# Masks by TensorE and sums by VectorE for the second batch's local head pairs, with a newly searched order

## The chip, the cores and the metric

The kernel runs on one core of a Trainium2 chip. The metric is the device time in microseconds of one execution of the whole program. A core has five engines with queues of their own: PE (TensorE, matrix products; its weight loads are listed as PEld), DVE (VectorE), ACT (ScalarE), POOL (GpSimd) and SP, which here only issues DMAs. Each engine takes its instructions strictly in the order in which they were emitted.

## What is computed

Eight batches of attention with eight heads each (576 positions, head size 64), and behind it a gated feed-forward block with a spatial product over the positions:

```python
scores = scale * np.matmul(q, k.transpose(0, 1, 3, 2))
mask_local = (rel >= 0) & (rel < stride)                       # stride = 32, heads 0 to 3
mask_strided = (rel >= 0) & (pos[None, :] % stride == pos[:, None] % stride)   # heads 4 to 7
scores = np.where(masks, scores, -1000000000.0)
attn = np.exp(scores - max); attn = attn / (sum(attn) + 1e-09)
x = (attn @ v) with the heads side by side                     # (8, 576, 512)
h = np.maximum(x @ w_in, 0.0); u, v = halves of h
v_n = (v - mean(v)) / np.sqrt(var(v) + 1e-06)
v_s = np.einsum('ts,bsd->btd', w_spatial, v_n) + b_spatial
out = (u * v_s) @ w_out
```

## The kernel before

**Tiles and stages.** Heads are handled in pairs: batch b has four pairs t = 4b to 4b+3, of which the first two are local and the last two strided. `attention(t, due)` (L695) loads q, k and v of a pair and calls `local_attention` (L445) or `strided_attention` (L585). A local pair has 18 blocks of 32 queries by 64 keys, packed into five slots for each of the two heads, so ten slots u of 128x64; the scores (L460) go to two PSUM tiles, one for each head. The result x of a pair (128 x 576, as a rounded and a rest part) feeds `moe_1` (v part: L870, u part: L912), and that feeds `moe_2` (spatial product L993, with the tail rows at L1005 and L1006; projection L1035). Every large product is made of three rounded products, high by high, high by low and low by high, so each weight is split once into a rounded part (`rnd`, L360: L368 on ACT, L370 on DVE or POOL) and a rest (`rest`, L374: L378). w_in and w_out arrive as 64-bit words and are first converted (L746 on ACT, L754 on POOL or L751 on DVE, L762 on DVE).

**Masks and softmax of a local pair.** There are two ways. For pairs in `PE_MASKED`, which are the first batch's four (0 to 3), TensorE adds the masks before the scores (`mask_scores`, L428: minus the unit matrix times the negated masks, L434, from the tile `at_minus`); VectorE takes the maxima of five slots at once (L480), scales them (L488), and ScalarE takes exp straight from PSUM (L517). For the others VectorE adds the mask slot by slot into SBUF, with the maximum as accumulated output (L497, ten instructions, each with a read of the accumulator), and ScalarE takes exp from there. For pairs in `APART` (0 and 1) the sums are a reduction by VectorE (L531); for the others exp writes its sum as well, which adds one accumulator read after each exp. Then come the normalising (L413, L417, L422), a transpose (L541), copies into `ptl` (L368, L370), the product with v (L570) and the split of x (L390 or L392, L378). The strided pairs have their own lines: scores L603, L619 or the mask by TensorE, L628, L634, exp L640, L645, the normalising, L657, copies into `pts`, product L673.

**The order.** Nothing is scheduled by hand. `Program.add` records each operation with a key (a due time in us on a scale of its own; smaller is more urgent), the engines that could do it with a cost in ns, and what it depends on. `Program.order` (L169) plays these through on modelled engines and a modelled DMA (310 bytes per ns, `DMA_RATE`): a free engine takes the ready operation with the smallest key. The engines' instructions are then emitted in the order of the modelled start times, and SP's DMAs too. `KEYS` (L40) holds the keys of the early work: a for the due times of pairs 0 to 7, v and u for the two halves of w_in (four row blocks each), o for w_out, s for the spatial weights, t for their tail, cst for the masks and the unit matrix, fill for the zeroed tiles; lead moves the due times of the pairs from batch 2 on. `fillers` (L280) puts products with zeros (L1168) ahead of PE operations before which the model sees PE idle for over 700 ns.

**Buffers that matter here.** Rings are reused in order, and a user of a slot waits for all earlier users of it: q and k two slots each, v_raw two, the PSUM tiles s two (local pairs from pair 4 on take both), m four, po two, o two. `at_minus`, which holds the negated unit matrix and masks, is the second slot of the ring o, so the second output tile of the first projection waits for the last mask product.

Of the kernel before, what the change touches and what calls it, by code (L numbers as in the profile page):

```python
# [23 lines left out]
STRIDE = 32  # L24
# [13 lines left out]
TAIL = S - 4 * P  # L38
NT = 4
KEYS = {  # L40
    "a": (-1127.3, -1221.6, -672.3, -526.1, 101.7, 33.0, 113.1, 239.5,),
    "v": (-238.9, -1399.6, -76.4, -73.7,),
    "u": (-43.5, -131.3, -12.3, -34.7,),
    "s": (684.8, 251.9, 2902.8, 2024.9,),
    "t": (1654.0,),
    "o": (6.6, -58.9, 103.7, 587.0,),
    "cst": (-1558.0,),
    "lead": (-1.36,),
    "fill": (50.5, 1235.4, -3578.4, 1164.7, -177.7, 809.5,),
    "dp": (849, -9544,),  # L50
    "dpt": (181.75,),
    "near": (198.57,),
}
WARM_END, WARM_GAP, WARM_COST, WARM_COLS, WARM_SHARE = 110000.0, 700.0, 427.0, 256, 0.8
PE_MASKED, APART = (0, 1, 2, 3), (0, 1)
OTHER_BANK = (1, 2, 3)
FETCHED, FETCH_COST = 200.0, 32.0
DMA_RATE = 310.0
# [4 lines left out]
PE, ACT, DVE, POOL, DMA = "tensor", "scalar", "vector", "gpsimd", "sync"  # L63
# [10 lines left out]
def local_blocks(slot):  # L74

    found = {}
    for i, n, first, c0, z in LOCAL_MOVES:  # L80
        if first <= slot < first + n:
            found[z] = 3 * (c0 + slot - first) + i
    return [found[z] for z in range(len(found))]
# [47 lines left out]
class Program:  # L131
# [7 lines left out]
    def add(self, key, choices, fn, reads=(), writes=(), spare=None, tiled=0, port=()):  # L139


        n = len(self.ops)
        if port:
            self.port[n] = port
        if spare is not None:
            self.spare[n] = spare
        if tiled:
            self.tiled[n] = tiled
        deps = set()
        for tok in reads:  # L150
            if tok in self.writer:
                deps.add(self.writer[tok])
            self.readers.setdefault(tok, []).append(n)
        for tok in writes:
            if tok in self.writer:
                deps.add(self.writer[tok])
            deps.update(self.readers.pop(tok, ()))
            self.writer[tok] = n
        for tok in (*reads, *writes):
            buf = tok[0]  # L160
            if isinstance(buf, Buf):
                deps.update(buf.before)
                if buf.n > buf.ring.bufs:
                    deps.update(buf.last.users[:1])
                buf.users.append(n)
        deps.discard(n)
        self.ops.append((key, choices, fn, deps))
# [142 lines left out]
def attention_moe(ctx, tc, qT, kT, vl, vs, cst, eye, w_in, w_out, wsp, wtail, out):  # L310
# [48 lines left out]

    def rnd(key, n, dst, src, reads, writes, engs=(ACT, DVE, POOL), blocks=False):  # L360

        cost = {ACT: 110 + 0.87 * n, DVE: 70 + 0.52 * n, POOL: 110 + 1.75 * n}
        if blocks:
            cost = {ACT: 200 + 0.85 * n, DVE: 175 + 0.5 * n, POOL: 175 + 0.9 * n}

        def fn(eng):
            if hasattr(eng, "activation"):
                eng.copy(dst(), src())  # L368
            else:
                eng.tensor_scalar(dst(), src(), 1.0, 0.0, op0=ALU.mult, op1=ALU.add)  # L370

        add(key, [(e, cost[e]) for e in engs], fn, reads, writes, port=(DVE,))

    def rest(key, n, dst, src, hi, reads, writes, engs=(DVE, POOL), extra=0):  # L374
        cost = {DVE: 70 + 1.04 * n + extra, POOL: 120 + 2.3 * n}

        def fn(eng):
            eng.tensor_tensor(dst(), src(), f32(hi()), op=ALU.subtract)  # L378

        add(  # L380
            key, [(e, cost[e]) for e in engs], fn, reads, writes,
            port=(DVE, POOL) if POOL in engs else (),
        )
# [12 lines left out]
    def load(key, dst, src, writes, nbytes, reads=()):  # L396
        add(key, [(DMA, nbytes / DMA_RATE)], lambda eng: eng.dma_start(dst(), src), reads, writes)
# [47 lines left out]
    def local_attention(t, due, q, kl, v, vin, kin):  # L445
# [45 lines left out]
        for u in range(nu):  # L491
            m = STRIDE * len(local_blocks(u // 2))
            f0 = 2 * STRIDE * (u // 2)
            msk = mask_l if u > 1 else mask_l0

            def f_m(eng, f0=f0, u=u, m=m, msk=msk):
                eng.tensor_tensor_reduce(  # L497
                    out=p_sb()[:m, u, :],
                    in0=s_ps[u % 2]()[:m, f0 : f0 + 2 * STRIDE],
                    in1=msk[:m],  # L500
                    scale=-SCALE,
                    scalar=3.0e38,
                    op0=ALU.add,
                    op1=ALU.min,
                    accum_out=st()[:m, u : u + 1],
                )

            if not masked:
                add(
                    due - 12.5, [(DVE, 75 + 1.04 * 2 * STRIDE)], f_m,  # L510
                    [(s_ps[u % 2],), ("cst",), ("local0", t % 2)], [(p_sb, u), (st, u)],
                )

            def f_e(eng, f0=f0, u=u, m=m):
                total = {} if t in APART else {"accum_out": st()[:m, NU + u : NU + u + 1]}
                src = s_ps[u % 2]()[:m, f0 : f0 + 2 * STRIDE] if masked else p_sb()[:m, u, :]
                eng.activation(  # L517
                    p_sb()[:m, u, :], src, AF.Exp,
                    bias=st()[:m, u : u + 1], scale=SCALE if masked else -1.0, **total,
                )  # L520

            add(
                due - 10, [(ACT, (95 if t in APART else 278) + 0.833 * 2 * STRIDE)], f_e,
                [(st, u), *([(s_ps[u % 2],), ("local0", t % 2)] if masked else [])],
                [(p_sb, u), (st, u)],
            )
# [36 lines left out]
        for c0 in (0, 3):  # L563
# [3 lines left out]
            def f_v(eng, c0=c0, o_ps=o_ps):  # L567
# [13 lines left out]
                due, x_t, o_ps, w, c0, lambda o_ps=o_ps, w=w: o_ps()[:, :w],  # L581
# [3 lines left out]
    def strided_attention(t, due, q, k, v, vin, kin):  # L585
# [73 lines left out]
        for i in range(4):  # L659
            r = slice(STRIDE * i, STRIDE * i + STRIDE)  # L660
            rnd(
                due - 5, nu * RA, lambda r=r, i=i: pts[r, :, i],
                lambda r=r: turned()[r, :, :RA], [(pc,), ("pts0",)], [("pts", i)], blocks=True,
            )
# [59 lines left out]
    def weight(key, src, n, dst, tok, stage):  # L724

        buf, i = stage
        if src.dtype == F32:
            val = lambda: buf().bitcast(F32).rearrange(FLAT[len(buf.ring.shape)])[:, 2 * i * n : 2 * i * n + n]
            load(key - 25, val, src, [(buf, i, 0), (buf, i, 1)], P * n * 4)
        else:
            raw = lambda dt: buf().bitcast(F32).rearrange(FLAT[len(buf.ring.shape)])[
                :, 2 * i * n : 2 * (i + 1) * n
            ].bitcast(dt)
            half = lambda j, dt=I32: raw(dt).rearrange("p (n t) -> p n t", t=2)[:, :, j]
            low, top = (buf, i, 0), (buf, i, 1)  # L740
            val = lambda dt=F32: half(1, dt)
            load(key - 25, lambda: raw(I32), src.bitcast(I32), [low, top], P * n * 8)

            add(
                key, [(ACT, 110 + 0.87 * n)],
                lambda eng: eng.activation(val(), val(), AF.Prelu, scale=2.0**-112, alpha=2.0**32),  # L746
                [], [top],
            )
            def lowest(eng):
                if hasattr(eng, "bn_stats"):  # L750
                    eng.tensor_scalar(half(0), half(0), 29, None, op0=ALU.logical_shift_right)  # L751
                else:
                    byte = raw(U8).rearrange("p (n t) -> p n t", t=8)[:, :, 3]
                    eng.tensor_scalar(half(0), byte, 1 / 32, -15.5 / 32, op0=ALU.mult, op1=ALU.add)  # L754

            add(
                key, [(DVE, 70 + 0.52 * n), (POOL, 110 + 1.8 * n)], lowest,
                [], [low], port=(DVE,),
            )
            add(  # L760
                key, [(DVE, 70 + 1.04 * n)],
                lambda eng: eng.scalar_tensor_tensor(  # L762
                    half(1), half(1), 3, half(0),
                    op0=ALU.logical_shift_left, op1=ALU.bitwise_or,
                ),
                [low], [top], port=(DVE,),
            )
        lo_in = [(buf, i, 0), (buf, i, 1)] if src.dtype == F32 else [top]
        rnd(key, n, lambda: dst(0), val, lo_in, [(*tok, 0)])
        rest(key, n, lambda: dst(1), val, lambda: dst(0), lo_in + [(*tok, 0)], [(*tok, 1)])  # L770

# [293 lines left out]
    lead = min(nb, 2)  # L1065
# [5 lines left out]
    cost = {1: 22.3, 0: 2.6, 2: 25.6}  # L1071
# [177 lines left out]
```

## Time and profile before

| | us |
|---|---|
| median of 3 runs (lowest to highest) | 529.07 (528.67 to 530.55) |
| the profiled execution, own time | 527.36 |
| its span, first to last instruction | 525.2 |
| PE, DVE, ACT, POOL busy | 509.7, 323.4, 236.9, 89.5 |

The time of an execution holds 2.16 us more than its span. The rows that are read stand below. A line "start, length, engine, line, operation, out<-in, shape, count" is a timeline row, with the idle time before it and what ended it in brackets; a waits row is "who line <- whom line: total us, times, longest". The busy time of DVE and ACT adds up instructions that overlap at their ends, so the distance from start to start is what a queue really pays.

### The profile page before, as it was taken

How to read it: one execution, taken by the hardware profiler on the slowest of the kernel's cores; microseconds unless marked ns; L12 is line 12 of the kernel's file. 1: busy time of each engine (PE TensorE's matmuls, PEld its weight loads, DVE VectorE, ACT ScalarE, POOL GpSimd, SP SyncE). 2: the span in 40 equal slices, each digit the busy share in tenths (PEclk: the TensorE clock that was granted, in tenths of full speed). 3: DMA queues.
4: the chain of work that ended last, by engine and by line, in shares of the span. 5: the costliest groups of instructions: out<-in, count | busy, mean ns of one | idle time of the engine just before them, and what ended most of it. 6: DMA issues, size and time to landing. Idle time of an engine off the chain costs nothing.

```text
span 525.2 us, 14576 instructions
## 1 busy us (share of the span) xinstructions
PE 509.7 (97%) x5982; PEld 468.7 (89%) x5982; DVE 323.4 (62%) x1020; ACT 236.9 (45%) x731; POOL 89.5 (17%) x176
## 2 busy tenths in 40 slices
PE   6898999999999999999999999999999999999997
PEld 3577799888998899988999899998999899998997
DVE  3999898695854868677246945868246353427132
ACT  6787856657546646343434335623312243213111
POOL 2463523121010302021010310102002020001000
PEclk9799999999999999999999999999999999999999
DMA  8779353632243233260223501321012200110011
GB/s 256 273 270 346 107 196 102 219 115 89 82 148 124 93 102 93 86 199 9 61 67 110 186 1 55 110 64 56 1 42 75 86 1 1 46 45 1 1 45 47
DMA packets 26242, 52.65 MB, mean 100 GB/s; under 512 B 3136, under 2 KB 11584, under 8 KB 26176
## 3 DMA queue, kind: packets, MB, share of 16 engines
q1 hardware_dynamic: 26176, 51.72, 30.0%
q8 instruction: 47, 0.77, 0.6%
q14 instruction: 19, 0.16, 0.1%
HBM read 42.27 MB, written 9.44 MB: 98 GB/s over the span
## 4 chain that ended last, share of the span: by engine, by line
PE 85%; DVE 7%; issue 2%; POOL 2%; ACT 1%; DMA 1%; SPq 0%; POOLq 0%; ACTq 0%; DVEq 0%
PE m L1035 20%; PE m L993 18%; PE m L870 17%; PE m L912 17%; PE po L673 3%; PE po L570 3%; PE s L460 2%; PE s L603 2%; PE m L1005 2%; PE m L1006 2%; DMA vn<-w_in 1%; POOL bn L846 1%; ACT pl L517 1%; POOL ptl L370 1%; DVE w_in_sb L378 1%
## 5 line engine op out<-in xcount | busy, mean ns | idle before, releaser
L993 PE MATMUL m<-wsp_sb,vn 128*128 128x288 f32 x768 | 111.6, 296 | 1.0 <-DVE wsp_sb L378 1.0
L1035 PE MATMUL m<-g,w_out_sb 128*128 128x288 f32 x768 | 107.8, 298 | 0.8 <-issue 0.5
L912 PE MATMUL m<-x,w_in_sb 128*128 128x288 f32 x768 | 105.4, 297 | 1.9 <-ACT vv L828 1.1
L993 PEld LDWEIGHTS m<-wsp_sb,vn 128*128 128x128 f32 x768 | 105.2, 189 | 2.1 <-DVE wsp_sb L378 1.2
L912 PEld LDWEIGHTS m<-x,w_in_sb 128*128 128x128 f32 x768 | 103.4, 188 | 3.5 <-ACT vv L828 1.3
L1035 PEld LDWEIGHTS m<-g,w_out_sb 128*128 128x128 f32 x768 | 103.6, 188 | 1.5 <-DVE g L378 0.5
L870 PE MATMUL m<-w_in_sb,x 128*128 128x512 f32 (+1 forms) x408 | 98.6, 397 | 0.2 <-DVE x L378 0.2
L870 PEld LDWEIGHTS m<-w_in_sb,x 128*128 128x128 f32 (+1 forms) x408 | 74.4, 185 | 20.3 <-issue 0.6
L390 ACT COPY o<-m 128x288 f32<-128x288 f32 x62 | 24.4, 396 | 106.0 <-PE m L1035 96.6
L1015 DVE TENSOR_TENSOR u<-m,u 128x288 f32<-128x288 f32 x64 | 28.1, 453 | 43.3 <-PE m L1006 42.9
L846 POOL TENSOR_TENSOR bn<-bn,sel 128x1 f32<-128x1 f32 (+1 forms) x37 | 21.9, 594 | 172.1 <-DVE bn L841 137.8
L370 POOL TENSOR_SCALAR ptl<-pc 32x320 f32<-32x320 f32 (+3 forms) x78 | 30.2, 388 | 122.4 <-PE po L570 63.7
L517 ACT ACTIVATE pl<-pl,ml 128x64 f32<-128x64 f32 (+1 forms) x140 | 47.0, 338 | 3.8 <-DVE ml L497 3.6
L926 ACT ACTIVATE u<-m 128x288 f32<-128x288 f32 x64 | 25.8, 410 | 49.2 <-PE m L912 49.0
L828 ACT ACTIVATE vv<-m 128x512 f32<-128x512 f32 (+1 forms) x37 | 22.1, 597 | 44.4 <-PE m L870 42.7
L378 DVE TENSOR_TENSOR x<-po,x 128x288 fp32r<-128x288 f32 x64 | 27.3, 448 | 22.5 <-ACT x L390 22.0
L833 DVE BATCH_NORM_STATS2 bn<-vv 128x6 f32<-128x512 f32 (+1 forms) x37 | 25.4, 687 | 20.8 <-ACT vv L828 20.6
L392 DVE CAST x<-po 128x288 fp32r<-128x288 f32 x14 | 6.2, 451 | 50.4 <-PE po L673 42.4
L853 DVE TENSOR_SCALAR vv<-vv,bn 128x512 f32<-128x512 f32 (+1 forms) x37 | 20.5, 557 | 18.0 <-POOL bn L846 18.0
L378 DVE TENSOR_TENSOR g<-u,g 128x288 fp32r<-128x288 f32 x63 | 28.0, 458 | 3.3 <-ACT g L368 2.1
L370 POOL TENSOR_SCALAR pts<-pc 32x288 f32<-32x288 f32 x29 | 15.4, 531 | 83.3 <-PE po L673 46.2
L517 ACT ACTIVATION_READ_ACCUMULATOR pl<-pl,ml 128x1 f32 (+1 forms) x140 | 26.4, 188 | 0.0
(121 smaller groups left out, 590.2 us busy)
## 6 DMA issues: line engine op xcount, KB each, us to landing
q<-qT SPq DMA_DIRECT2D x32, 295.0 KB, 4.3
outT<-o SPq DMA_DIRECT2D x64, 144.0 KB, 1.8
v_raw<-vs SPq DMA_DIRECT2D x15, 512.0 KB, 3.7
v_raw<-vl SPq DMA_DIRECT2D x16, 384.0 KB, 4.4
k<-kT SPq DMA_DIRECT2D x16, 304.0 KB, 4.7
kbd<-kT SPq DMA_DIRECT2D x32, 144.0 KB, 4.3
vn<-w_in SPq DMA_DIRECT2D x4, 512.0 KB, 5.3
u<-w_in SPq DMA_DIRECT2D x3, 512.0 KB, 6.9
```

The source lines that it names most:

```text
L370: eng.tensor_scalar(dst(), src(), 1.0, 0.0, op0=ALU.mult, op1=ALU.add)
L378: eng.tensor_tensor(dst(), src(), f32(hi()), op=ALU.subtract)
L390: eng.copy(dst(), src())
L517: eng.activation(p_sb()[:m, u, :], src, AF.Exp, bias=st()[:m, u : u + 1], scale=SCALE if masked else -1.0, **total,)
L833: lambda eng: eng.bn_stats(bn()[:m, 0:6], v()[:m]), [(v,)], [(bn,)],
L846: lambda eng: eng.tensor_tensor(bn()[:m, 9:10], bn()[:m, 8:9], sel[:m, 0:1], op=ALU.pow),
L870: eng.matmul(v_ps()[:m, :], x_at(kt)[:, a, :], w_in_sb[:, w, kt, HF:], start=(n == 0 and i == 0), stop=(n == NT - 1 and i == 2),)
L912: eng.matmul(u_ps()[:, :HS], w_in_sb[:, w, kt, f * P : (f + 1) * P], xs[NHP * b + kt]()[:, a, r], start=(n == 0 and i == 0), stop=(n == NT ...
L926: lambda eng, u=u, f=f, u_ps=u_ps: eng.activation(u()[:, f * HS : (f + 1) * HS], u_ps()[:, :HS], AF.Relu),
L993: eng.matmul(s_ps()[:, :HS], vn()[:, a, kt, fs], wsp_sb[:, w, kt, r], start=(kt == 0 and i == 0), stop=False,)
L1015: lambda eng, ug=ug, s_ps=s_ps: eng.tensor_tensor(ug(), s_ps()[:, :HS], ug(), op=ALU.mult),
L1035: eng.matmul(o_ps()[:, :HS], w_out_sb[:, w, f, e * P : (e + 1) * P], g[a]()[:, f, :], start=(f == 0 and i == 0), stop=(f == NT - 1 and i = ...
```

## The change

Pairs 4 and 5, the second batch's local pairs, join `PE_MASKED` and `APART`: their masks are added by TensorE, their maxima and sums taken by VectorE in whole reductions, and exp reads PSUM and has no accumulated output. Three modelled ACT costs are raised (rounding and Prelu from 110 to 122 ns of fixed cost, exp of a pair in `APART` from 95 to 142), and all numbers in `KEYS` are others. The code that makes the instructions is not touched otherwise.

```diff
 KEYS = {
-    "a": (-1127.3, -1221.6, -672.3, -526.1, 101.7, 33.0, 113.1, 239.5,),
-    "v": (-238.9, -1399.6, -76.4, -73.7,),
-    "u": (-43.5, -131.3, -12.3, -34.7,),
-    "s": (684.8, 251.9, 2902.8, 2024.9,),
-    "t": (1654.0,),
-    "o": (6.6, -58.9, 103.7, 587.0,),
-    "cst": (-1558.0,),
-    "lead": (-1.36,),
-    "fill": (50.5, 1235.4, -3578.4, 1164.7, -177.7, 809.5,),
-    "dp": (849, -9544,),
-    "dpt": (181.75,),
-    "near": (198.57,),
+    "a": (-1015.2, -2680.2, -820.4, -905.7, 34.2, 48.1, 229.2, 305.1,),
+    "v": (-842.6, -1087.2, -549.5, -665.6,),
+    "u": (19.5, -740.5, 11.1, -99.6,),
+    "s": (1080.7, 2734.5, 1469.3, 1550.8,),
+    "t": (1863.0,),
+    "o": (65.6, 34.0, 94.4, 1273.9,),
+    "cst": (-1125.9,),
+    "lead": (7.79,),
+    "fill": (1513.1, 2745.6, -3875.0, 553.2, -1289.0, 971.6,),
+    "dp": (3934, -4967,),
+    "dpt": (307.75,),
+    "near": (288.54,),
 }
-PE_MASKED, APART = (0, 1, 2, 3), (0, 1)
+PE_MASKED, APART = (0, 1, 2, 3, 4, 5), (0, 1, 4, 5)
-        cost = {ACT: 110 + 0.87 * n, DVE: 70 + 0.52 * n, POOL: 110 + 1.75 * n}
+        cost = {ACT: 122 + 0.87 * n, DVE: 70 + 0.52 * n, POOL: 110 + 1.75 * n}
-                due - 10, [(ACT, (95 if t in APART else 278) + 0.833 * 2 * STRIDE)], f_e,
+                due - 10, [(ACT, (142 if t in APART else 278) + 0.833 * 2 * STRIDE)], f_e,
-                key, [(ACT, 110 + 0.87 * n)],
+                key, [(ACT, 122 + 0.87 * n)],
```

## Rows read from the trace of the kernel before

**Rows 1.** Stretches: start:end, length, busy us and (instructions) of PE, PEld, DVE, ACT, POOL, PEclk, DMA.
```profile
0.00:21.60 21.60, 15.49 (x329) 8.94 (x329) 12.41 (x35) 14.10 (x40) 5.45 (x15) 0.84 0.76 255
21.60:40.00 18.40, 17.54 (x148) 13.34 (x148) 17.81 (x37) 14.97 (x31) 12.42 (x16) 1.00 0.83 283
40.00:72.00 32.00, 29.09 (x478) 25.80 (x476) 29.44 (x94) 24.51 (x80) 14.27 (x23) 1.00 0.60 208
72.00:521.60 449.60, 447.60 (x5034) 420.65 (x5032) 263.76 (x857) 182.87 (x581) 57.38 (x123) 1.00 0.24 78
```

**Rows 2.** The same view, 0 to 72 us, L1168 alone (products with zeros).
```profile
0.00:72.00 72.00, 10.06 (x24) 3.51 (x24) 0.95 0.71 241
```

**Rows 3.** Waits of PE, whole span.
```profile
PE po L673 <- issue: 1.2, 1, 1.2
PE m L912 <- ACT vv L828: 1.1, 1, 1.1
PE m L993 <- DVE wsp_sb L378: 1.0, 1, 1.0
...
PE m L912 <- DVE w_in_sb L378: 0.4, 1, 0.4
```

**Rows 4.** Timeline of PE: masks of pairs 1 and 0, first large product, pairs 5 and 4.
```profile
6.12 0.73 PE L434 MATMUL m<-o 128*128 128x64 f32 x4
...
7.14 0.45 PE L434 MATMUL m<-o 128*128 128x288 f32 x2
...
21.59 1.66 PE L870 MATMUL m<-w_in_sb,x 128*128 128x512 f32 x6
...
40.49 0.97 PE L460 MATMUL s<-k,q 64*32 64x64 f32 x72
...
58.16 0.97 PE L460 MATMUL s<-k,q 64*32 64x64 f32 x72
...
63.23 3.69 PE L993 MATMUL m<-wsp_sb,vn 128*128 128x288 f32 x26 [0.98 <-DVE wsp_sb L378]
```

**Rows 5.** DVE: two neighbouring old masks (timeline), then three links of the chain, pairs 1 and 0.
```profile
48.98 0.22 DVE L497 CUSTOM_DVE_ANT_0 pl<-s,cst_sb 128x64 f32<-128x64 f32 x1
49.12 0.08 DVE L497 DVE_READ_ACCUMULATOR2_ANT ml<- 128x1 f32 x1
49.12 0.22 DVE L497 CUSTOM_DVE_ANT_0 pl<-s,cst_sb 128x64 f32<-128x64 f32 x1
...
9.29 0.80 DVE ml L480 x2
12.40 0.82 DVE ml L531
14.21 0.11 DVE ml L488 x2
```

**Rows 6.** Timeline of ACT: ten exps of pair 1; third and last exp of pair 5.
```profile
10.26 2.11 ACT L517 ACTIVATE pl<-m,ml 128x64 f32<-128x64 f32 x10 [1.70 <-DVE ml L488]
...
50.90 0.34 ACT L517 ACTIVATE pl<-pl,ml 128x64 f32<-128x64 f32 x1
...
53.23 0.33 ACT L517 ACTIVATE pl<-pl,ml 64x64 f32<-64x64 f32 x1
```

**Rows 7.** Waits of SP, 0 to 72 us.
```profile
SPq L397 <- PE po L570: 13.8, 2, 8.0
...
SPq L397 <- DVE w_in_sb L378: 10.2, 1, 10.2
```

**Rows 8.** Timeline of DVE: three instructions of a strided pair of the second batch.
```profile
73.61 0.45 DVE L619 SCALAR_TENSOR_TENSOR pp<-s,cst_sb 128x288 f32<-128x288 f32 x1
...
77.20 0.25 DVE L417 RECIPROCAL mx<-mx 128x16 f32<-128x16 f32 x1
...
78.23 0.70 DVE L657 STREAM_TRANSPOSE pc<-pp 128x512 f32<-128x512 f32 x1
```

**Rows 9.** Timeline of ACT: the first output tile of the first projection.
```profile
74.40 0.40 ACT L390 COPY o<-m 128x288 f32<-128x288 f32 x1 [1.12 <-PE m L1035]
```

## The prediction

> **What bounds the kernel now.** I first read the stretches of the span [rows 1]. [...] The last 3.6 us are the last output. What is left is the first 72 us. PE is idle there for 6.1 + 0.9 + 2.9 = 9.9 us [rows 1] and spends 10.0 us on products with zeros [rows 2], so some 20 us carry no work. Most of these lie before the first large product at 21.59 us [rows 4], when the first pair's chain from its loads to its x has to run through once; the granted clock of that stretch is 0.84, so part of it ran at the lower level. From 21.6 to 72 PE is idle for 0.9 + 2.9 = 3.8 us, and DVE is busy for 17.81 of 18.40 and for 29.44 of 32.00 us [rows 1]: **the ramp is bound by DVE**, and PE's longest waits there end on ACT's work or DVE's splits (1.1, 1.0 and 0.4 us) [rows 3].
>
> So the answer has a frame: a perfect order of the same work saves 3.8 us in the ramp and 2.0 behind it, plus what could be taken out of the first 21.6 us, where the chain of one pair decides more than the order of the rest.
>
> **The edits, one by one.** Each is worked out for one pair and then doubled.
>
> *PE, masks.* Four mask tiles (two of pair 1, two of pair 0), eight products, run from 6.12 to 7.14 us, which is 1.02 us [rows 4]. Pairs 4 and 5 add as many, so **+1.0 us of PE work**. Whether it costs time depends on where it lands. The scores of these pairs run at 40.49 and 58.16 us, and PE waits soon behind each of them, 0.98 us at 63.23 behind the second [rows 4]. Such waits end on DVE and ACT [rows 3], so the masks fall into time that PE would have waited. I cost them at 0, with 1.0 as the upper end if the waits go.
>
> *DVE.* Removed are ten L497 with their accumulator reads, which start 0.14 us apart (48.98 and 49.12) [rows 5], so 1.4 us. Added are two maxima, 0.80 together, two scalings, 0.11, and the sum, 0.82 [rows 5]: 1.73 us. That is **+0.3 us for a pair, +0.6 for two**, on the engine that bounds the ramp. The other end comes from the lengths of the rows, where an old mask is 0.22 + 0.08 us and ten of them 3.0 [rows 5]: by that a pair would save 3.0 - 1.7 = 1.3 us, two 2.6. I take the start-to-start distance, since the accumulator read runs beside the next mask, and keep -2.6 as the lower end.
>
> The trace shows the old masks packed at 0.14 us [rows 5]. [...]
>
> *ACT.* From the third to the last exp of pair 5 are seven steps in 53.23 - 50.90 us, 0.33 each with the accumulated sum, so ten are 3.3 us; ten without a sum take 2.11 us from PSUM [rows 6]. So **-1.2 us for a pair, -2.4 for two**. ACT is busy for 24.51 of 32.00 us in that stretch [rows 1], so it isn't the bound; what it can give back is PE's wait on it, 1.1 us [rows 3]. I book -0.5, between 0 and -1.1.
>
> *Buffers.* Exp now reads PSUM, so both tiles of s are held until the last exp and not until the last mask. The last exp of pair 5 ends at 53.56 [rows 6] and the next scores that need them come at 58.16 [rows 4]: 4.6 us of cover. The second output tile of the first projection now waits for the last masks as well; the first tile is copied at 74.40 [rows 9], and the last scores, ahead of which the masks stand, ran by 59.1 [rows 4], which covers 15 us. Both cost 0. If that cover went, ACT would stand at the output copy, with the rounding of g and x queued behind it.
>
> The edits alone: 0 + 0.6 - 0.5 = **+0.1 us**, between -3.7 and +1.6.
>
> **The new order.** Its times can't be read off the keys, only its tendency. The first pair (1) still comes first and the first row block of w_in's v half second, so the head of the chain keeps its shape. The other v blocks (-842, -549, -665 where they were -239, -76, -74) move up among pairs 2 and 3, which lets conversions use time in which DVE stands: it is busy for only 12.41 of the first 21.60 us [rows 1]. Pair 3 now precedes pair 2; its v tile still needs the slot of pair 1, and SP stood in front of such slots for 13.8 us in two waits on L570, the longest 8.0, every later load behind them [rows 7]. Raising ACT's modelled cost lets the model release such slots later, nearer to the trace: exps of pairs 0 and 1 were modelled at 95 + 53 = 148 ns, now 195, and take 2.11 / 10 = 211 [rows 6]. So the queue should stand less on waits that the model didn't see. SP also stood 10.2 us for one stage buffer [rows 7], but the DMA engines were busy for 0.83 of 21.6 to 40 [rows 1], so little of that was lost. The pairs from batch 2 on are pulled forward by 9.15 (lead), in a stretch that has 2.0 us to win.
>
> The order's bounds are thus 0 to -5.8; what a worse one costs is the second rival. I take half of the ramp's idle time, 1.9, and a fifth of the 2.0 behind it, 0.4: **-2.3 us**. The half is a choice: the waits end on different engines, and where one goes, DVE's next split becomes the late one.
>
> **Sum.** +0.1 - 2.3 = -2.2 us: span 525.2 to 523.0, own time 527.36 to 525.2. The profiled execution is 1.71 us under the median, so on the median's scale 529.07 - 2.2 = **526.9 us**, 0.4% less. A measurement of this kernel can tell about 0.5%, 2.6 us, from no change.
>
> **Rivals.**
>
> 1. *The order takes all it can.* The ramp's idle time and the issue wait go, -3.8 - 1.2, and the edits give -0.3: -5.3 us, **523.8**. For it: the waits are few and each at one place [rows 3], and DVE has 9 us free before 21.6 [rows 1]. Against: DVE is full from 21.6 on. Chance 0.36.
>
> 2. *Slower: the spatial weights come late.* Their keys move from 685, 252, 2903, 2025 to 1081, 2735, 1469, 1551, while pairs 6 and 7 stand at 229 and 305, so DVE may do these pairs' work first. Already PE stands 0.98 us at 63.23 for a split of the spatial weights [rows 4], so there is no margin: every us by which the last split that this run needs moves past 63.2 is lost, since the second batch's large products can't start before all its pairs are done. The price is one strided pair's work on DVE, eight instructions: five like L619 of 0.45, two like L417 of 0.25 and a transpose of 0.70 [rows 8], 3.45 us at most. With the +0.6 of the edits it is +4.0: **533.1**. Against: the old keys stood in the same sequence for three of the four blocks, and pairs 6 and 7 must find their loads and slots first. Chance 0.20.
>
> 3. *The order moves waits about and removes none.* Then only the edits count: +0.1, **529.2**. Chance 0.14.
>
> **How the numbers follow.** Forecast 0.30, rivals 0.36, 0.20 and 0.14. The forecast and rival 3 lie within 0.5% (526.4 to 531.7): same 0.44. Faster by more 0.36, slower by more 0.20. The likeliest of the three signs is no change that can be told, and its likeliest value is the forecast. The range runs from rival 1 with 1.3 us, half of the DVE term's lower end, to rival 2: 522.5 to 533. It leaves out a gain in the first 21.6 us and a second strided pair ahead of the spatial weights. The likeliest case alone would be 525.5 to 529.
>
> **What the next profile would show.** Right: L497 starts only with the third batch's pairs, L434 grows by eight products, L480 has eight rows and L531 four, exps of pairs 4 and 5 stand about 0.21 us apart; PE is idle for about 2 us between 21.6 and 72, the first large product stays near 21.6, and the stretch behind 72 stays full. Wrong: a first large product well before or after 21.6, a wait of PE for wsp_sb of over 1 us, or ACT standing at the second output tile. The sum rests most of all on PE's work from 72 us on being the same.

## The result and the profile after

The changed kernel takes **531.64 us** (median of 20 runs, 530.0 to 533.3) beside 529.51 us for the kernel before on the same chip. The ratio is **1.0039**, 95% interval 1.0022 to 1.0056: slower by 0.4%, where 0.4% faster was forecast. The time lies in the range and within the 0.5% that was called no change; the sign was wrong. The profiled execution takes 530.0 us with a span of 528.1, 2.9 longer than before.

The stretches of after, in the columns of [rows 1]; the last row begins where the second batch's large products are about to start and ends with the last of PE's work:

```profile
0.00:21.60 21.60, 15.80 (x332) 10.52 (x333) 11.18 (x28) 15.13 (x42) 8.67 (x21) 0.84 0.82 279
21.60:40.00 18.40, 17.49 (x148) 13.21 (x147) 18.25 (x38) 14.67 (x31) 11.51 (x19) 1.00 0.87 291
40.00:72.00 32.00, 28.95 (x465) 26.46 (x465) 28.53 (x60) 21.67 (x58) 10.99 (x18) 1.00 0.48 163
97.00:524.00 427.00, 423.72 (x4616) 396.60 (x4605) 221.75 (x707) 181.81 (x555) 63.32 (x139) 1.00 0.22 72
```

The corresponding stretch of before:

```profile
97.00:521.00 424.00, 422.26 (x4673) 396.42 (x4672) 244.06 (x774) 168.41 (x527) 52.78 (x112) 1.00 0.23 74
```

Where two instructions of an engine overlap, the busy times of these rows count that time once, for DVE and ACT too; only the mean length in a group's row counts each instruction in full.

In the ramp hardly anything moved: from 21.6 to 72 us PE is idle for 0.9 + 3.1 = 4.0 us, where it was 3.8. DVE is busy for 0.9 us less from 40 to 72, ACT for 2.8 less. In the late part, where the prediction saw up to 2.0 us to win and nothing to lose, PE is now idle for 427.00 - 423.72 = 3.3 us; before it was 424.00 - 422.26 = 1.7.

The waits of PE in after, whole span, as [rows 3]:

```profile
PE m L603 <- DMA kbd<-kT: 2.1, 2, 1.9
PE m L870 <- ACT u L926: 1.6, 1, 1.6
PE s L434 <- ACT pl L517: 1.5, 1, 1.5
PE m L912 <- issue: 1.1, 1, 1.1
PE m L1005 <- DVE tail L378: 1.1, 1, 1.1
PE m L1035 <- issue: 1.0, 1, 1.0
...
PE po L673 <- issue: 0.9, 1, 0.9
```

The wait for wsp_sb has gone (1.0 before), and so has that for w_in_sb; in their place PE stands for u, for a pair's pl and for tail. Three waits for *issue* of 1.1, 1.0 and 0.9 us are new; before there were two, 1.2 and 0.5. PE's timeline in after around the three:

```profile
116.71 1.22 PE L673 MATMUL po<-pts,v_raw 128*64 128x72 f32 x32
117.86 1.49 PE L603 MATMUL s<-kbd,q 128*32 128x36 f32 x128
119.28 0.67 PE L912 MATMUL m<-x,w_in_sb 128*128 128x288 f32 x3
121.04 1.20 PE L912 MATMUL m<-x,w_in_sb 128*128 128x288 f32 x7 [1.09 <-issue]
...
164.16 0.30 PE L1035 MATMUL m<-g,w_out_sb 128*128 128x288 f32 x1
165.50 0.67 PE L1035 MATMUL m<-g,w_out_sb 128*128 128x288 f32 x3 [1.05 <-issue]
...
341.89 1.21 PE L570 MATMUL po<-ptl,v_raw 128*64 128x96 f32 x24
343.03 1.38 PE L603 MATMUL s<-kbd,q 128*32 128x36 f32 x128
344.34 0.60 PE L673 MATMUL po<-pts,v_raw 128*64 128x72 f32 x12
345.83 0.85 PE L673 MATMUL po<-pts,v_raw 128*64 128x72 f32 x20 [0.89 <-issue]
```

None of them stands at the start of a tile that another engine writes: PE stops *inside* a series of equal products, a few behind or within a long **run** of small ones (24 of L570, 128 of L603 and 32 of L673, 184 in all, or some of these). Behind 95 us, after has four runs of 184 and two of 160 such products, before three of 184 and two of 160.

To place the loss over the whole span I added up, group by group of PE's timeline, the distance from one start to the next minus what the group's products take at the full granted clock, as the traces of before and after have it from start to start (0.2335 us for one of L870, 0.1333 for one of L912, L993, L1005, L1006 or L1035, 1.14 for 24 of L570, 1.15 for 32 of L673, 0.9 for 72 of L460, 0.7 for 64 of L603; masks and products with zeros count as lost). The times for one product are rounded, so the sum serves to compare kernels and not as an exact loss. The sum so far, in us:

```
up to us    22    40    60    72    97   110   125   168   240   300   360   500
before    17.5  19.4  23.2  24.2  24.4  24.5  24.6  24.9  26.3  26.8  26.7  26.4
after     17.9  19.5  22.3  24.4  24.6  25.1  26.7  28.5  27.9  27.8  29.7  29.7
```

**Up to 97 us it is a tie** (24.6 to 24.4, the new masks included), as far as one execution can tell: executions below with the same order up to there give 25.7 and 26.0 for after and 25.6 for before. Behind it before loses 2.0 us and after 5.1, in steps at 121, 165 and 346 us (1.4, 1.2 and 1.1 us), where the issue waits are, and 0.6 at 335 us, where L1035 stands 0.25 us for DVE's g.

### The profile page after: what moved, and what is told of

It is laid out like the page before. It is cut to its first block, busy times and chain, and to the rows that moved or that the text cites. A ratio compares the mean times of both kernels' runs of the same rounds, so it can differ in the third digit from the quotient of the medians.

```text
span 528.1 us, 14533 instructions
## 1 busy us (share of the span) xinstructions
PE 511.4 (97%) x5990; PEld 470.9 (89%) x5990; DVE 297.8 (56%) x907; ACT 250.6 (47%) x754; POOL 103.0 (20%) x216
## 3 DMA queue, kind: packets, MB, share of 16 engines
q1 hardware_dynamic: 26176, 51.72, 29.7%
## 4 chain that ended last, share of the span: by engine, by line
PE 84%; DVE 8%; POOL 3%; issue 2%; DMA 1%; ACT 1%; SPq 0%; POOLq 0%; DVEq 0%; ACTq 0%
PE m L1035 20%; PE m L993 18%; PE m L912 17%; PE m L870 17%; PE po L673 3%; PE po L570 3%; POOL ptl L370 2%; PE s L460 2%; PE m L1005 2%; PE s L603 2%; PE m L1006 2%; DMA vn<-w_in 1%; DVE w_in_sb L378 1%; DVE bn L833 1%; POOL bn L846 1%
## 5 line engine op out<-in xcount | busy, mean ns | idle before, releaser
L993 PE MATMUL m<-wsp_sb,vn 128*128 128x288 f32 x768 | 114.1, 297 | 0.0
L1035 PE MATMUL m<-g,w_out_sb 128*128 128x288 f32 x768 | 107.2, 297 | 1.3 <-issue 1.0
L912 PE MATMUL m<-x,w_in_sb 128*128 128x288 f32 x768 | 105.7, 297 | 1.5 <-issue 1.1
L993 PEld LDWEIGHTS m<-wsp_sb,vn 128*128 128x128 f32 x768 | 105.7, 189 | 1.5
L912 PEld LDWEIGHTS m<-x,w_in_sb 128*128 128x128 f32 x768 | 103.5, 188 | 3.0 <-issue 1.3
L1035 PEld LDWEIGHTS m<-g,w_out_sb 128*128 128x128 f32 x768 | 103.8, 188 | 2.4 <-issue 1.3
L870 PE MATMUL m<-w_in_sb,x 128*128 128x512 f32 (+1 forms) x408 | 99.1, 397 | 1.7 <-ACT u L926 1.6
L870 PEld LDWEIGHTS m<-w_in_sb,x 128*128 128x128 f32 (+1 forms) x408 | 74.1, 185 | 21.4 <-ACT u L926 1.8
L390 ACT COPY o<-m 128x288 f32<-128x288 f32 x63 | 25.1, 398 | 87.5 <-PE m L1035 75.0
L846 POOL TENSOR_TENSOR bn<-bn,sel 128x1 f32<-128x1 f32 (+1 forms) x37 | 20.7, 560 | 191.1 <-DVE bn L841 157.0
L370 POOL TENSOR_SCALAR ptl<-pc 32x64 f32<-32x64 f32 (+3 forms) x101 | 40.3, 399 | 76.8 <-PE po L570 50.5
L926 ACT ACTIVATE u<-m 128x288 f32<-128x288 f32 x64 | 25.7, 410 | 44.7 <-PE m L912 43.7
L517 ACT ACTIVATE pl<-pl,ml 128x64 f32<-128x64 f32 (+1 forms) x120 | 40.4, 340 | 3.1 <-DVE ml L497 2.8
L370 POOL TENSOR_SCALAR pts<-pc 32x288 f32<-32x288 f32 x40 | 19.4, 485 | 91.0 <-PE po L673 65.2
L368 ACT COPY ptl<-pc 32x320 f32<-32x320 f32 (+3 forms) x85 | 29.9, 352 | 5.8 <-DVE pc L541 4.3
L390 ACT CAST x<-po 128x288 fp32r<-128x288 f32 x60 | 22.7, 396 | 19.8 <-PE po L570 12.9
```

Source lines behind the costliest of these rows:

```text
L517: eng.activation(p_sb()[:m, u, :], src, AF.Exp, bias=st()[:m, u : u + 1], scale=SCALE if masked else -1.0, **total,)
L846: lambda eng: eng.tensor_tensor(bn()[:m, 9:10], bn()[:m, 8:9], sel[:m, 0:1], op=ALU.pow),
L870: eng.matmul(v_ps()[:m, :], x_at(kt)[:, a, :], w_in_sb[:, w, kt, HF:], start=(n == 0 and i == 0), stop=(n == NT - 1 and i == 2),)
L912: eng.matmul(u_ps()[:, :HS], w_in_sb[:, w, kt, f * P : (f + 1) * P], xs[NHP * b + kt]()[:, a, r], start=(n == 0 and i == 0), stop=(n == NT ...
L993: eng.matmul(s_ps()[:, :HS], vn()[:, a, kt, fs], wsp_sb[:, w, kt, r], start=(kt == 0 and i == 0), stop=False,)
L1035: eng.matmul(o_ps()[:, :HS], w_out_sb[:, w, f, e * P : (e + 1) * P], g[a]()[:, f, :], start=(f == 0 and i == 0), stop=(f == NT - 1 and i = ...
```

## Experiments

The theory: the runs of small products cost the time, since PE's instructions arrive too late. Rivals: the edits cost it, or the ramp, or waits that happen to fall there because of the order or the loads. All ratios are to the kernel before on the same chip, with 95% intervals.

### The change again, its order alone, its edits alone

After once more, unchanged, beside the later experiments:

> The changed kernel itself, as the measure for the three runs beside it: 1.002 to 1.006 of before, with two or three waits for issue of about 1 us behind 97 us.

531.11 us, **1.0035** (1.0011 to 1.0059), as expected. The three waits stand at the same places (122.25, 167.11 and 347.49 us), 1.03, 1.41 and 0.77 us long; the sum above is 25.7 at 97 and 30.9 at 500 us.

The order alone, with the edits undone:

```diff
-PE_MASKED, APART = (0, 1, 2, 3, 4, 5), (0, 1, 4, 5)
+PE_MASKED, APART = (0, 1, 2, 3), (0, 1)
```

> The changed kernel with its keys and costs, but pairs 4 and 5 masked and summed the old way: the new order without the edits. From 97 us on its TensorE order has the same long runs of small products as the changed kernel. Theory A (the edits are hidden in the ramp, the loss of 2.1 us lies behind 97 us, in waits for issue of about 1.1 us each after runs of 160 and more small products): as slow as the changed kernel, 1.003 to 1.005 of before. Rival B (the edits cost, 1.0 us of masks on TensorE and 0.6 us of VectorE): 1.6 us faster than the changed kernel, 1.000 to 1.002 of before.

530.07 us, **1.0018** (0.9997 to 1.0039). The time alone decides nothing: 1.0018 lies in the range that was expected if the edits cost the time, 1.000 to 1.002, and not in the theory's, 1.003 to 1.005, and the interval reaches from no loss to all of it. The trace speaks for the order. The sum is 25.1 at 97 us and 29.7 at 500, so 4.6 us are lost late, where after loses 5.1 and before 2.0. PE waits for issue behind 97 us in three places:

```profile
122.02 9.60 PE L912 MATMUL m<-x,w_in_sb 128*128 128x288 f32 x70 [0.28 <-issue]
281.66 0.27 PE L603 MATMUL s<-kbd,q 128*32 128x36 f32 x6 [0.23 <-issue]
346.37 0.60 PE L673 MATMUL po<-pts,v_raw 128*64 128x72 f32 x12 [1.34 <-issue]
```

So the late loss comes with the new order, without the edits too. By these ratios the edits add 0.0017, 0.9 us, with intervals that overlap; after's issue waits are longer than these by 3.03 - 1.85 = 1.2, so nothing of a size that can be told is left for the edits' own work. (Without the eight mask products all that follows also stands 16 instructions earlier, which can move the waits, as shown below.)

Before with the edits under the old keys, and with its long runs cut as in the next section:

```diff
-PE_MASKED, APART = (0, 1, 2, 3), (0, 1)
+PE_MASKED, APART = (0, 1, 2, 3, 4, 5), (0, 1, 4, 5)
```

> The kernel before with the edits alone (pairs 4 and 5 masked by TensorE and summed by VectorE; keys and costs of before, order made anew from them), and the runs of small products cut behind 95 us as in the runs beside it. To be held against before with runs cut. Theory A: equal within 0.5 us. Rival B: 1.6 us slower.

539.78 us, **1.0207** (1.018 to 1.0233). Neither of the two expected outcomes came, and this doesn't tell the edits' cost: the planner places everything anew, and what it found from the old keys is poor. Waits of PE behind 95 us:

```profile
PE s L460 <- DVE ml L497: 2.2, 1, 2.2
PE s L460 <- DMA kbd<-kT: 1.8, 1, 1.8
PE m L870 <- DVE x L392: 0.9, 1, 0.9
PE m L870 <- DVE x L378: 0.8, 1, 0.8
```

At 97 us its sum is 25.0, near before's 24.4; the loss comes behind that, with these waits.

### No long runs

First by a cut in PE's order alone: behind 95 us a run of at least 150 small products is parted, and up to six large products that follow it, and whose inputs the plan has ready, go into its middle.

```diff
-        fillers = self.fillers(issued)
+        fillers, issued = self.fillers(issued), apart(self, issued)
...
+        if sum(sizes) >= 150 and start[pe[k]] > first:
+            half = pe[k + next(i for i in range(run) if sum(sizes[: i + 1]) > 96)]
+            for n in pe[k + run : k + run + most]:
+                if n in tiled or any(d not in taken and ends[d] > start[half] for d in ops[n][3]):
+                    break
+                taken.append(n)
```

> The changed kernel, with the TensorE order alone changed behind 95 us: where 150 or more small products (L460, L570, L603, L673) follow each other, up to six large ones that are ready are taken from behind the run into its middle; nothing else moves. Theory A: the waits for issue of 1.1, 1.0 and 0.9 us go, 2 to 3 us less than the changed kernel, 0.998 to 1.001 of before. Rivals B (the edits cost) and C (the new start costs, by a lower granted clock or a later first product): no change against the changed kernel, 1.003 to 1.005 of before.

After with this cut: 536.47 us, **1.0156** (1.013 to 1.0183). A miss, since the waits have gone (0.3 us is left) and others are there:

```profile
PE m L1035 <- DVE g L378: 2.6, 6, 1.1
PE m L1035 <- ACT g L368: 1.9, 4, 1.0
```

Most likely the small products now end later, what DVE and ACT do with them stands late in their queues, and the splits of g behind it come late for the output projection; only the waits themselves are shown. An order changed on one engine only doesn't test a wait fairly.

> The kernel before with the same cut of its runs of small products behind 95 us (three of 184, two of 160). Theory A: its waits for issue, 1.2 and 0.5 us in the trace, go: 0.996 to 0.998 of before. Rivals B and C: no change, 0.999 to 1.001.

Before with the same cut: 527.19 us, **0.9967** (0.9951 to 0.9983), no issue wait left, 1.4 us lost behind 97 us where it was 2.0.

Then by the planner itself, so that all engines follow. It keeps a stock of small products that PE may run in a row, at most 200, and 32 ns bring one back (numbers of its model, not of a trace); behind 95 us the cap is set to 100, which makes another order of all engines from there on:

```diff
-                stock = min(FETCHED, stock + (now - since) / FETCH_COST)
+                stock = min(FETCHED if now < 95000.0 else 100.0, stock + (now - since) / FETCH_COST)
```

> The changed kernel with one number of its planner: behind 95 us the modelled stock of fetched small products fills up to 100 and not to 200, so the planner itself (all engines, not TensorE alone) never lets more than about 128 of them follow each other. Up to 95 us the order is the changed kernel's. Theory A (the loss lies behind 97 us in waits for issue after long runs): the waits go and no waits for DVE take their place, as they did where TensorE alone was cut; 2 to 3 us less than the changed kernel, 0.998 to 1.000 of before. Rivals B (the edits) and C (the start): as slow as the changed kernel.

After so: 528.56 us, **0.998** (0.9957 to 1.0003), beside 1.0035 for after on the same chip: 2.6 us less. One run of 160 is left, at 97 us, where the order is still after's; PE passes it without a wait. The late loss is 2.0 us, as much as before's.

> The kernel before, planned anew with a cap of 100 instead of 200 on the planner's stock of small products behind 95 us, so that no run of 184 or 160 follows there. The two waits (1.2 and 0.5 us) vanish: ratio 0.996 to 0.998. Against the kernel after with the same cap (0.998) it tells what the masks, the sums and the new keys do up to 97 us: if their ramp is worth the 2.3 us that was predicted, this one is 2 us slower than that; if the ramp is a tie or a loss, it is equal to it or up to 1 us faster.

Before so: 526.29 us, **0.9946** (0.9926 to 0.9965), the fastest of all, 2.3 us below before, and more than was expected (0.996 to 0.998, the two waits of 1.2 and 0.5 us). PE from 97 us on, in this kernel and then in the last one:

```profile
97.00:521.00 424.00, 424.00 (x4683) 397.10 (x4682) 245.84 (x769) 170.66 (x540) 56.30 (x114) 1.00 0.23 75
```

```profile
97.00:522.00 425.00, 424.75 (x4704) 396.95 (x4703) 224.66 (x713) 180.31 (x547) 63.55 (x141) 1.00 0.23 73
```

PE is idle for 0.00 and 0.25 us, where before had 1.7 and after 3.3. With the waits gone from both, the new keys and edits are 0.0034, 1.8 us, slower than the old ones (each against before on its own chip; the intervals overlap by 0.0008). The expectation set a gain of the 2.3 us that I had predicted against a tie or a loss of up to 1 us in the ramp; it is a loss, and by the sum mostly a late one: 0.4 us up to 97 (26.0 to 25.6), less than executions of one order differ there, and 1.6 behind it (2.0 to 0.4), of which 0.9 lie around 335 us, where L1035 stands for g as in after.

### Blocks of 256 instructions

All the late waits for issue have one thing in common. I counted PE's records in the trace (products, weight loads and what its sequencer has) ahead of each wait, and looked at the transfers of queue q8, which the page of after lists as

```profile
q8 instruction: 47, 0.77, 0.6%
```

Each of the 47 packets has 16,384 bytes; with 12,085 records (5,990 products, 5,990 weight loads and 105 of the sequencer) that is one packet for 257. The profile doesn't say whose instructions these are; that they are PE's, 256 records to a packet, is read from this count and the times below. The waits behind 97 us, from the records (a block's time runs from the first of its starts to the last):

```
kernel  wait ends  records ahead      the 256 ahead  last packet        PE goes on
before     229.74  6593 = 25*256+193  took 2.09 us   227.06 to 228.28   1.46 us later
before     293.92  8129 = 31*256+193       3.56      291.66 to 292.54   1.38
after      121.04  3777 = 14*256+193       1.76      118.38 to 119.44   1.60
after      165.50  5057 = 19*256+193       3.74      163.25 to 164.22   1.28
after      345.82  9409 = 36*256+193       1.57      343.53 to 344.57   1.25
```

The two rows of before, as the timeline has them:

```profile
229.74 0.34 PE L673 MATMUL po<-pts,v_raw 128*64 128x72 f32 x3 [1.20 <-issue]
...
293.92 0.30 PE L1035 MATMUL m<-g,w_out_sb 128*128 128x288 f32 x1 [0.54 <-issue]
```

Every wait stands 193 records into a count by 256, at the seam of two blocks, and PE goes on 1.25 to 1.6 us after the end of a packet. From 100 us on a block takes 11.7 us on average (36 in 421 us). One that lies all in a run of small products is through in 1.6 to 2.1 us, one that lies in it for the most part in 3.6 to 3.7, and if its successor hasn't come by then, PE stands. Where it had, PE doesn't: after runs through the block from 280.00 to 281.73 us, whose successor's packet ended at 280.03, without a wait.

The same count over all 14 traces (before, after and the twelve runs), 46 seams each, bears it out. No seam is passed sooner than 1.21 us after the end of the packet that belongs to it. Of their 34 waits for issue over 0.15 us, 31 stand at a seam; the other three (0.23, 0.89 and 0.30 us, between 73 and 80 us) stand ahead of a series of L460, and their cause stays open.

If that is right, where the waits stand depends on how the runs lie to the seams, and moving the seams, with order and work as they are, must move the waits. Each product with zeros is two products and two weight loads in the trace (12 in the program, 24 of either in [rows 2]); cut into four narrower ones it has as many columns and 12 instructions more.

```diff
+    pieces = [4, 4, 4, 4, 4, 4, 2]
     def warm(buf, count):
         for _ in range(count):
-            nc.tensor.matmul(
-                buf()[:STRIDE, :WARM_COLS], zeros,
...
+            k = pieces.pop(0) if pieces else 1
+            for _ in range(k):
+                nc.tensor.matmul(
+                    buf()[:STRIDE, : WARM_COLS // k], zeros,
```

> The kernel before; the first six of its twelve zero products are cut into four of 64 columns and the seventh into two of 128, same columns in all, so that all that follows stands 76 TensorE instructions (38 products and their 38 weight loads) later in the instruction stream; order and work unchanged. Theory (TensorE's stream comes in blocks of 256 instructions; a run of over 150 small products waits when it takes up a whole block before the next one has come): waits put down to issue near 101, 181, 289 and 351 us, perhaps at 227, instead of the two at 230 and 294 us, of 0.7 to 1.5 us each, and the time 2 to 5 us above before (1.004 to 1.010). Rival (the waits come from something else at these places, the order or the loads): waits where they were, time as before, within 0.3%.

531.67 us, **1.0053** (1.003 to 1.0076), 2.8 us slower for 76 instructions in the idle start. The rows of PE's timeline behind 97 us that begin with a wait for issue:

```profile
102.86 0.40 PE L603 MATMUL s<-kbd,q 128*32 128x36 f32 x22 [0.55 <-issue]
184.68 0.32 PE L603 MATMUL s<-kbd,q 128*32 128x36 f32 x11 [1.14 <-issue]
293.68 1.09 PE L673 MATMUL po<-pts,v_raw 128*64 128x72 f32 x27 [0.96 <-issue]
357.66 2.56 PE L1035 MATMUL m<-g,w_out_sb 128*128 128x288 f32 x18 [1.72 <-issue]
```

Near the four places that were named (101, 181, 289 and 351 us; they came 2 to 7 us later), again 193 records into their block; the wait at 230 us has gone. The third stands at nearly the time of before's wait at 293.92, but in another series, L673 and not L1035, since the seam has moved. PE is idle for 428.00 - 423.63 = 4.4 us from 97 to 525. The rival, that waits hang on the order or the loads, falls.

> The kernel after; eight of its twelve zero products are cut into four and two into two, so that all that follows stands 104 TensorE instructions later; order and work unchanged. Theory of the blocks: the waits at 121 and 346 us vanish, the one near 161 to 165 us stays, a new one near 98 us is likely: two waits instead of three, and 0.5 to 1.5 us less than after (ratio 1.000 to 1.003). Rival (waits hang on order or loads): the three waits stay where they are, ratio 1.0035 as for after.

After, eight products cut into four and two into two: 531.81 us, **1.0055** (1.003 to 1.0081). Half a hit:

```profile
103.68 0.53 PE L673 MATMUL po<-pts,v_raw 128*64 128x72 f32 x9 [1.21 <-issue]
...
227.68 1.06 PE L993 MATMUL m<-wsp_sb,vn 128*128 128x288 f32 x6 [0.61 <-issue]
```

The waits at 121 and 346 us are gone and the one near 98 us has come, but that of 165 us has shrunk out of the list and one at 227 us is there. The late loss fell as expected, from 5.1 to 3.7 us, but the median didn't: in this profile the sum is already 29.0 at 97 us. Much of that seems to come from the moved seams, since two of them now have waits in the ramp, where the expectation hadn't looked:

```profile
12.56 0.30 PE L460 MATMUL s<-k,q 64*32 64x64 f32 x4 [0.83 <-issue]
...
22.29 0.45 PE L603 MATMUL m<-kbd,q 128*32 128x36 f32 x10 [2.18 <-issue]
...
26.63 2.02 PE L870 MATMUL m<-w_in_sb,x 128*128 128x512 f32 x6
```

Both waits stand 193 records into their block (a third, of 0.38 us, at 76.12 too). The cut products with zeros also end 1.2 us later than the uncut ones in after, and the first large product comes at 26.63 us, 4.4 us later than in after, by as much as the sum has grown. The granted clock from 21.6 to 40 us is 0.84 where after has 1.00. Of the 12 executions 7 had a mean granted clock of 0.988 or less, of the 12 of after again 2; what share of that the cut products have was not tried.

### The terms of the sum

The masks of pairs 4 and 5 four times over (eight products become 32, 3.1 us more by [rows 4]):

```diff
-                mask_scores(due, o_ps, ((0, 2 * STRIDE, 1), (1, 2 * STRIDE, LS - 1)))
+                mask_scores(due, o_ps, ((0, 2 * STRIDE, 1), (1, 2 * STRIDE, LS - 1)), 1 + 3 * (t in (4, 5)))
```

> The changed kernel with the mask products of pairs 4 and 5 issued four times (24 products more, 3.1 us by the rate of the first masks; the sum of masks stays far below any score, so the result is the same). If the masks lie in time that TensorE would have waited (my step): 0 to 1 us more than the changed kernel. Rival B (they lie on the path): 3.1 us more.

530.33 us, **0.9999** (0.9976 to 1.0023), less than after. That doesn't show that masks are free: the 48 more instructions moved the seams, one of the three late waits is left (166.07 us, 0.97), and the late loss falls by 2.1 us to 2.9. The time fell by only 0.8 against after's median, so some 1.3 of the 3.1 us are paid in the ramp (in the profile the sum at 97 us is 28.6, 2.9 to 4.0 above after's two; 0.6 of it is an issue wait at 84.50, at a seam as well, and the granted clock is lower too, 0.79 and 0.96 in the first two stretches). With seams, clock and masks mixed, this run gives the masks' cost only roughly.

The maxima and sums of pairs 4 and 5 on DVE twice:

```diff
-                    lambda eng, j=j: eng.tensor_reduce(
+                    lambda eng, j=j: [eng.tensor_reduce(
...
+                    ) for _ in range(1 + (t in (4, 5)))],
```

> The changed kernel with the maxima and the sums of pairs 4 and 5 taken twice on VectorE (3.2 us more of its work in the ramp; same result). If VectorE bounds the ramp as I put it: 2 to 3 us more than the changed kernel, and the +0.6 us that I booked for the edit were on the path. If there is cover: under 1 us more.

533.03 us, **1.0061** (1.0036 to 1.0086), 1.9 us above after on the same chip, for four L480 of 0.48 and two L531 of 0.81 us, 3.5 us. The late loss is 4.7, near after's 5.1, so this is the ramp: a little over half of DVE's work there is on the path (by the medians, with an uncertainty of over 1 us; the profiled execution loses 29.9 us up to 97, at a granted clock of 0.81 and 0.95 in the first two stretches, so it doesn't serve for this).

The exps of pairs 4 and 5 with their accumulated sums, as ScalarE made them before:

```diff
-                total = {} if t in APART else {"accum_out": st()[:m, NU + u : NU + u + 1]}
+                total = {} if t in (0, 1) else {"accum_out": st()[:m, NU + u : NU + u + 1]}
```

> The kernel after in its own order, but the eight exponentials of pairs 4 and 5 also write their sums, as ScalarE did before (VectorE's sums still overwrite them): some 0.12 us more for each of the eight with the read of the accumulator, 1.0 to 2.4 us more of ScalarE in 45 to 72 us. If ScalarE's time there is on the path as I took it (half of it), 0.5 to 1.2 us slower than after (ratio 1.0045 to 1.006); if other engines end the waits, as after (1.0035).

532.25 us, **1.0061** (1.0038 to 1.0083). It is ten exps for each of the two pairs, so twenty, not eight; ACT is busy for 23.65 instead of 21.67 us from 40 to 72, 2.0 more. Against after's 1.0035 that is 1.4 us, somewhat above the 0.5 to 1.2 expected; the two intervals overlap, so the cost isn't clear of zero.

## Why the prediction was wrong

**The failed step is the order's -2.3 us.** The order alone measured +0.9 (1.0018; its interval, -0.2 to +2.1 us, has room for no change but not for a gain of 2.3), and the whole change +2.1. Both halves of the term failed.

- *The 0.4 behind 72 us, and the frame "2.0 behind it".* The 2.0 are the 449.60 - 447.60 us for which PE is idle there [rows 1]. This took the stretch as one that could only gain. It treated the issue wait at L673, 1.2 us of the 2.0 [rows 3], as a delay that a better order sheds, and never asked what makes it, or how many more of its kind a new order could have. The lines "near", "dp" and "lead" of the diff are just what arranges small products around the large ones behind 72 us. I gave them a sentence. No rival had a price for a loss there, though the prediction ended by saying that the sum rested on this. The late part lost 3.1 us by the traces: issue waits (3.0 us instead of 1.7) and the step at 335 us (0.6) make up 1.9 of it; the rest is in steps below 0.5 us that I can't name.
- *The 1.9 in the ramp.* Nothing was won: PE is idle for 4.0 us from 21.6 to 72 instead of 3.8, and the first large product comes at 22.23 us instead of 21.59 [rows 4]. The waits ended on other things than before, as rival 3 had it ("moves waits about and removes none").

**The edits** were about right. From after, the lines of DVE's new work, the first large product, ACT's exps of pair 5, and PE's masks of pairs 4 and 5:

```profile
L480 DVE TENSOR_REDUCE ml<-s 128x5 f32<-128x320 f32 x4 | 1.8, 480 | 0.1
L531 DVE TENSOR_REDUCE ml<-pl 128x10 f32<-128x640 f32 x2 | 1.6, 807 | 0.0
L488 DVE TENSOR_SCALAR ml<-ml 128x5 f32<-128x5 f32 x4 | 0.4, 150 | 0.0
```

```profile
22.23 1.67 PE L870 MATMUL m<-w_in_sb,x 128*128 128x512 f32 x6
```

```profile
64.53 2.10 ACT L517 ACTIVATE pl<-s,ml 128x64 f32<-128x64 f32 x10
```

```profile
16.13 1.22 PE L434 MATMUL s<-o 128*128 128x64 f32 x4 [1.53 <-ACT pl L517]
...
59.41 0.62 PE L434 MATMUL s<-o 128*128 128x64 f32 x4
```

- *Masks, 0, bound 1.0.* Pair 5's stand beside its scores, as thought. Pair 4's went to 16.13 us, ahead of them by 26 us and behind a wait of 1.53 us for the s tile's release by the exps. So the place was wrong for one pair. By the experiment with 3.1 us more, some four tenths are paid: 0.4 for the change, between the two ends.
- *DVE, +0.6.* The added work is 1.8 + 1.6 us with four scalings of 0.4 together, so 3.8 where I had 3.46 (the maxima take a little longer, and I took 0.11 us for both scalings of a pair, which take 0.2). Less the 2.8 of the old masks that is +1.0 us of work, and a little over half counts, by the doubled reductions, so some +0.5.
- *ACT, -0.5.* Ten exps take 2.10 us, as read from pair 1 (2.11). Putting the sums back cost 1.4 us, which would make half too little, but that is within the uncertainty.
- *Buffers, 0.* Right: ACT's copy of the first output tile stands at 74.55 us (74.40 before), and nobody waits for it.

Together the edits come to about -0.5 by these three runs, each with an uncertainty of over 1 us; neither the +0.1 forecast nor the +0.9 of after against the order alone lies outside that.

**Rival 2**, spatial weights late, had the right sign (533.1) by a mechanism that isn't there: L993 doesn't wait for wsp_sb at all in after. That the time lies in the range is luck: the range's upper end is this rival's sum, and the likeliest case alone ended at 529. **Rival 1** fell: the issue waits grew; no run shows its -0.3 for the edits: by the rows of after DVE's work grew by 1.0 us, and the three runs give the edits some -0.5, each with an uncertainty of over 1 us. Of the prediction's own tests, "the stretch behind 72 stays full" was the one that failed.

**Settled:** the late waits come from runs of small products at the seams of PE's instruction blocks; taking the runs away takes the waits away in both kernels (none behind 97 us with the cap of 100), moving the seams moves them, and no seam in any trace is passed sooner than 1.21 us after its packet. **Open:** what the new order does in the ramp, below the 1.4 us by which executions of one order differ there; and the 1.8 us by which the new keys and edits stay behind with all runs short; part of it is a wait for g near 335 us, the rest wasn't tried.

## What to carry to other kernels

A stretch in which the bounding engine is 99.6% busy can still lose time (PE's was 447.60 of 449.60 us [rows 1], and after lost 3.1 us more behind 97), so a change of order needs a rival there too: read each short wait in it, above all those that no data explain, and ask what makes it and how many more places could have it. Where a wait falls inside a series of equal instructions, count the instructions ahead of it; a planner that allows 200 small products in a row counts one where the trace has two records, a product and its weight load (5,990 of either in after). A tuned kernel may owe a microsecond or two to where its instructions happen to lie (before lost 2.8 us when 76 more stood ahead of them), so in an experiment that adds instructions the waits at the seams, early ones too, have to be read before its time is taken as the cost of the work.

## What the hardware showed that I had not expected

- Queue q8 brought 47 packets of 16,384 bytes in before as in after, beside 12,075 and 12,085 records of PE; 31 of the 34 waits for issue over 0.15 us in 14 traces stand 193 records into a count by 256. So PE's instructions seem to come in blocks of 256 during the run. Behind 97 us, PE had to wait 0.2 to 1.7 us for the next block behind some of those that were through in 1.4 to 4.3 us; the runs of 160 and 184 products (320 and 368 instructions with their weight loads) are long enough for that. With the stock capped at 100, PE was idle for 0.00 us of 424 in one kernel.
- 76 instructions more at the start of the stream, at unchanged order and columns, cost before 2.8 us in all; 104 more in after came with waits of 0.83 and 2.18 us at seams in the first 23 us.
- Executions of one kernel differ by the mean granted clock: of the 35 executions of before beside the last experiments, 21 at 0.992 or more average 528.2 us, 3 at 0.988 or less 531.6. Whether the clock makes the time or idle time the clock isn't shown.
